# Talking heads attention with a gated MLP on one core: the first head mix of two groups at once, on four 64x64 tiles

## Chip, cores and metric

The kernel runs on one core of a Trainium2 chip. The metric is the device time of one execution in microseconds (us). Views of the trace count from the first instruction of the profiled execution.

## The reference

Four batches, 12 heads, 448 positions, head size 64. Two mixes over heads stand around the softmax; the result goes through a gated MLP with a residual.

```python
scores = scale * np.matmul(q, k.transpose(0, 1, 3, 2))
scores = np.einsum('bhij,hg->bgij', scores, w_pre)        # first head mix
scores = scores - np.max(scores, axis=-1, keepdims=True)
attn = np.exp(scores)
attn = attn / (np.sum(attn, axis=-1, keepdims=True) + 1e-09)
attn = np.einsum('bhij,hg->bgij', attn, w_post)           # second head mix
attn_out = np.matmul(attn, v)
...
h = gelu(x @ w_in); u, v = halves of h; v_n = layer norm of v, times g_ln
v_s = np.einsum('ts,bsd->btd', w_sg, v_n) + b_sg[None, :, None]
return x + (u * v_s) @ w_out
```

## The kernel before

Most fp32 values are carried as a high and a low fp16 part, so that a product takes several fp16 matmuls that add up in PSUM.

**Scores.** The 448 query rows of a batch are cut into chunks of 120, 120, 88 and 120 rows. For each chunk and head two matmuls (`qk_mm`, L674 and L675) give 120 x 448 scores. ScalarE or VectorE casts them to a high fp16 part (`qk_hi`, L695 through the helper at L291 or L293), VectorE computes the low part (`qk_lo`, L700), and for every two heads `write` (L706) sends both to a buffer `s1_d` in DRAM. There the rows of one query are 12 high rows, then 12 low rows. The first chunk of all (`N_Q32` = 1) keeps its scores in fp32 instead (L709).

**Groups.** Ten query rows are a group; a chunk has 12 groups, or 9. `load_pair` (L764) brings two groups back into one of three buffers `g`: a group as two halves of five query rows, each half with 5 x 2 x 12 = 120 partitions (query row, high or low, head). All these transfers are issued by SyncE (SP), in order.

**First head mix.** `premix` (L782) multiplies by a block matrix of `w_pre`: 120 rows, and 60 columns of 64. For each of the high and low parts of the weights and each half, one fp16 matmul of 448 columns goes to its 64 partitions of one PSUM bank (L792). The products low x low are in it, so there are four terms. In the fp32 chunk one full fp32 matmul does a group (L788).

**Softmax and second mix.** VectorE takes the maximum (`softmax_max`, L797), ScalarE the exponential with its sum (L804), VectorE the reciprocal (L809, L810). For the first 45 groups only the second weights are normalized (`w_norm`, L812) and an fp32 matmul mixes (L847); later groups are normalized and split into high and low parts, mostly on GpSimd (L293, L296), and mixed by fp16 matmuls of 64 rows that write two banks of `at2` (`postmix`, L857). Attention times v (`av`, L973) and the MLP of the batch (L1008) follow.

**Order.** `Plan` writes the order of all engines while the kernel is built: every step is a generator that yields an engine, a cost in ns, a rank (about the number of the group) and conditions; the planner picks by earliest start and rank. `slot(n)` (L880) holds the steps of group n, and adds the next group's once its own mix is placed. The two score banks (`ps_s2`, two buffers) serve the groups in turn:

```python
t = yield "pe", 746 if i < N_Q32 else 421, n - 3.5, 0, lambda: after([seen(("pair", pair_of[n])), past("exp", n - 2)])
premix(n)
```

Of the kernel before, what the change touches and what calls it, by code (L numbers as in the profile page):

```python
# [85 lines left out]
def talking_heads_gmlp(ctx, tc, q, k, v, w_pre, w_post, w_in, g_ln, w_sg, b_sg, w_out, out):  # L86
# [48 lines left out]
    wpre_hi = const.tile([2 * NH * H, 64], F16, name="wpre_hi")  # L135
    wpre_lo = const.tile([2 * NH * H, 64], F16, name="wpre_lo")
    wrep = const.tile([P, 2, H], F32, name="wrep")
    msk = const.tile([P, 5, NH], F32, name="msk")
# [14 lines left out]
    gring = [const.tile([2 * NH * H, 4, S], F16, name=f"g{i}") for i in range(RING)]  # L153
    vn_hi = const.tile([P, NCH, DH], F16, name="vn_hi")
    wfull = vn_hi.rearrange("p c f -> p (c f)")[:NT * H, 128:384].bitcast(F32)
    wpc32 = vn_hi.rearrange("p c f -> p (c f)")[:, 384:504].bitcast(F32)
    mskc_t = vn_hi.rearrange("p c f -> p (c f)")[:, 504:520].bitcast(F32)
    wpre32 = vn_hi.rearrange("p c f -> p (c f)")[:NT * H, :128].bitcast(F32)
# [21 lines left out]
    s1_d = [dram.tile([CQ * 2 * H, S], F16, name=f"s1_d{i}") for i in range(3)]  # L180
# [496 lines left out]
    def qk_full(i, h, ps, eng=None):  # L677
        ev = min(CQ, q_rows(i)[1])
        qk_place(i, h)
        e = ebox[i, h // 2 * 2].rearrange("p t u j -> p (t u j)").bitcast(F32).rearrange("p (u j) -> p u j", u=2)  # L680
        cast(e[:ev, h % 2, :], ps[:ev, :S], 1.0 / math.sqrt(D), eng)

    def qk_place(i, h):
        if h % 2 == 0:
            if (i, h) in early:
                ebox[i, h] = early[i, h].rearrange("p (t u j) -> p t u j", t=2, u=2)
# [16 lines left out]
    def s1_full(i):
        return s1_d[i % 3].rearrange("(q t) j -> q (t j)", t=2).bitcast(F32)
# [56 lines left out]
    def g_full(p):  # L761
        return gring[p % RING].rearrange("p u j -> p (u j)").bitcast(F32).rearrange("p (u j) -> p u j", u=2)

    def load_pair(p):  # L764
        i, t, n = pairs_[p]
        ng = min(2, GROUPS[chunks[i][1]] - t)
        r0 = t * NT * 2 * H
        if i < N_Q32:
            r0 = t * NT * H
            src = s1_full(i)[r0:r0 + ng * NT * H, :].rearrange("(u m) j -> m u j", m=NT * H)  # L770
            nc.sync.dma_start(out=g_full(p)[:, :ng, :], in_=src)
            return
        src = s1_d[i % 3][r0:r0 + ng * NT * 2 * H, :].rearrange("(u m) j -> m u j", m=2 * NH * H)
        nc.sync.dma_start(out=gring[p % RING][:, :2 * ng, :], in_=src)
# [4 lines left out]
    def cstart_end(i):  # L779
        return cstart[i] if i < len(chunks) else NG  # L780

    def premix(n):  # L782
        g = gring[pair_of[n] % RING]
        u = 2 * (glist[n][2] % 2)
        ps = ps_s2.tile([P, 512], F32, tag="s2", name="ps_s2")
        st[n] = {"s2": ps}
        if n < cstart_end(N_Q32):
            nc.tensor.matmul(ps[:, :S], lhsT=wfull, rhs=g_full(pair_of[n])[:, glist[n][2] % 2, :], start=True, stop=True)  # L788
# [718 lines left out]
```

## Time and profile before

| | us |
|---|---|
| three executions, median | 692.51 |
| their lowest and highest | 688.84, 981.43 |
| the profiled execution | 688.67 |
| its span, first to last instruction | 686.9 |
| TensorE busy, share of the span | 623.3 (91%) |
| VectorE, ScalarE, GpSimd busy | 474.7, 467.5, 416.7 |
| mean granted TensorE clock | 0.973 |

One of the three executions, 981.43, lies far from the other two. A matmul's duration in the profile holds its way through the array, so durations of neighbours overlap; the distance from one start to the next tells what a matmul costs the engine. `PE` is TensorE's matmuls and `PEld` its weight loads, `DVE` is VectorE, `ACT` ScalarE, `POOL` GpSimd, and `SPq` is the sequencer of SyncE, which issues the transfers.

### The profile page before, as it was taken

The page shows a single profiled execution, that of the slowest core. Times are in us where ns is not written, and L with a number is a line of the kernel's source. Part 1 is how long each engine was busy: PE and PEld are TensorE (multiplying, and loading weights), DVE is VectorE, ACT ScalarE, POOL GpSimd, SP SyncE. Part 2 cuts the span into 40 slices and gives each one's busy share as a digit, 9 for nine tenths or more (in the row PEclk, how much of TensorE's full clock was granted, in tenths as well). Part 3 has the DMA queues.
Part 4 walks back from the last instruction along what each step waited for, and adds up shares of the span by engine and source line. Part 5 has one row for each costly group of instructions (what it writes and reads, how often), then busy time and mean ns, then how long its engine had stood idle before and what let it go on. Part 6 is the DMA issues. An engine that isn't in the chain of part 4 may idle for free.

```text
span 686.9 us, 21481 instructions
## 1 busy us (share of the span) xinstructions
PE 623.3 (91%) x8589; PEld 415.2 (60%) x8589; DVE 474.7 (69%) x1073; ACT 467.5 (68%) x1037; POOL 416.7 (61%) x560
## 2 busy tenths in 40 slices
PE   6598798879779897999999998999899999999997
PEld 3355565557546644766675654775665746767776
DVE  5677998878799876756769667556768686344670
ACT  4557686768779786666778787766779696664311
POOL 5043685565679866676778767776676768773000
PEclk8889999999989998899999999999999999999999
DMA  8799999999989599766979399967887394540022
GB/s 194 211 267 277 276 269 240 279 217 293 290 231 247 129 235 248 187 189 158 280 173 239 98 249 254 194 190 201 233 176 192 103 266 129 145 130 29 1 94 80
DMA packets 152290, 135.57 MB, mean 197 GB/s; under 512 B 65646, under 2 KB 144814, under 8 KB 152190
## 3 DMA queue, kind: packets, MB, share of 16 engines
q1 hardware_dynamic: 151929, 134.19, 78.4%
q8 instruction: 67, 1.10, 0.7%
q14 instruction: 34, 0.27, 0.1%
q10 hardware_dynamic: 260, 0.01, 0.0%
HBM read 77.01 MB, written 47.87 MB: 182 GB/s over the span
## 4 chain that ended last, share of the span: by engine, by line
PE 54%; DMA 20%; DVE 12%; issue 5%; POOL 5%; ACT 3%; SPq 0%; POOLq 0%; ACTq 0%; DVEq 0%
PE ps_x L1008 10%; PE ps_av L973 7%; PE ps_s L792 7%; PE at L857 6%; PE ps_u L1008 5%; DMA g<-s_d 5%; PE ps_v L1008 5%; DMA qT<-q 5%; PE ps_qk L674 4%; PE ps_qk L675 3%; DMA s_d<-s 3%; DMA st<-in_moe_w_out_dram 2%; DVE s L700 2%; DVE nm L797 2%; PE at L847 2%
## 5 line engine op out<-in xcount | busy, mean ns | idle before, releaser
L797 DVE TENSOR_REDUCE nm<-ps_s 128x1 f32<-128x448 f32 x180 | 110.1, 615 | 42.7 <-PE ps_s L792 34.8
L296 POOL TENSOR_TENSOR pl<-p,ph 128x448 f16<-128x448 f32 x123 | 129.9, 1058 | 8.7 <-ACT ph L291 2.8
L804 ACT ACTIVATE p<-ps_s,nm 128x448 f32<-128x448 f32 x180 | 113.1, 629 | 27.1 <-DVE nm L797 24.0
L291 ACT ACTIVATE at<-at 112x480 f32<-112x480 f32 x180 | 109.8, 612 | 18.5 <-PE at L857 10.4
L700 DVE SCALAR_TENSOR_TENSOR s<-ps_qk,s 120x448 f16<-120x448 f32 (+1 forms) x172 | 105.9, 617 | 16.3 <-ACT s L291 14.0
L291 ACT ACTIVATE s<-ps_qk 120x448 f16<-120x448 f32 (+2 forms) x169 | 91.2, 542 | 21.7 <-PE ps_qk L675 19.3
L973 PE MATMUL ps_av<-at,v 112*64 112x120 f32 (+1 forms) x1536 | 83.6, 267 | 5.2 <-DVE s L700 3.1
L674 PE MATMUL ps_qk<-kT,qT 128*128 128x448 f16 (+1 forms) x192 | 71.7, 374 | 16.1 <-DVE xTl L986 11.2
L973 PEld LDWEIGHTS ps_av<-at,v 112*64 112x64 f32 x1536 | 77.5, 141 | 10.8 <-DVE s L700 3.7
L293 POOL TENSOR_SCALAR p<-p,rs 128x448 f32<-128x448 f32 x74 | 49.7, 672 | 46.9 <-DVE rs L810 28.4
L857 PEld LDWEIGHTS <-ph 64*128 64x128 f16 x2160 | 49.8, 94 | 41.6 <-issue 27.8
L792 PE MATMUL ps_s<-g,wpre_hi 120*64 120x448 f16 x336 | 64.5, 379 | 10.4 <-DMA g<-s_d 9.6
L293 POOL TENSOR_SCALAR ph<-p 128x448 f16<-128x448 f32 x100 | 59.4, 594 | 21.0 <-PE at L857 7.4
L675 PE MATMUL ps_qk<-kT,qTs 128*128 128x448 f16 (+1 forms) x192 | 69.8, 364 | 0.0
L1008 PE MATMUL ps_u<-xTh,wbuf 128*128 128x120 f16 (+1 forms) x768 | 63.6, 215 | 1.1 <-DVE gl_v L1052 1.1
L1008 PEld LDWEIGHTS <-wbuf 128*128 128x128 f16 x1152 | 59.3, 99 | 8.5 <-issue 5.7
L857 PE MATMUL at<-wpc_hi,ph 64*128 64x60 f16 x1080 | 61.4, 191 | 2.1 <-ACT at L291 2.0
L792 PE MATMUL ps_s<-g,wpre_lo 120*64 120x448 f16 x336 | 61.2, 359 | 0.0
L857 PE MATMUL at<-wpc_hi,pl 64*128 64x60 f16 x1080 | 59.9, 188 | 0.7 <-POOL pl L296 0.7
L857 PE MATMUL at<-wpc_lo,ph 64*128 64x60 f16 x1080 | 60.0, 188 | 0.0
L1008 PE MATMUL ps_u<-xTl,wbuf 128*128 128x120 f16 (+1 forms) x384 | 59.9, 215 | 0.0
L1008 PE MATMUL ps_x<-wbuf,gt_hi 128*120 128x384 f16 (+1 forms) x232 | 57.2, 329 | 0.0
(238 smaller groups left out, 1351.8 us busy)
## 6 DMA issues: line engine op xcount, KB each, us to landing
g<-s_d SPq DMA_DIRECT2D x88, 420.0 KB
s_d<-s SPq DMA_DIRECT2D x62, 420.0 KB
s_d<-s SPq DMA_DIRECT2D x24, 336.0 KB
wbuf<-wo_d SPq DMA_DIRECT2D x16, 384.0 KB
v<-in_v_dram SPq DMA_DIRECT2D x16, 336.0 KB
wbuf<-wu_d SPq DMA_DIRECT2D x12, 384.0 KB
out_dram<-ot SPq DMA_DIRECT2D x24, 180.0 KB
q<-in_q_dram SPq DMA_DIRECT2D x11, 384.0 KB
```

The costliest lines, as they stand in the source:

```text
L291: e.activation(out=o, in_=i, func=AF.Copy, scale=scale)
L293: e.tensor_scalar(out=o, in0=i, scalar1=scale, scalar2=1.0, op0=ALU.mult, op1=ALU.mult)
L296: (e or pl.on).tensor_tensor(out=o, in0=a, in1=b, op=ALU.subtract)
L674: nc.tensor.matmul(ps[:rows, :S], lhsT=qT2[i % 2][:, h, :rows], rhs=kT[:, h, :], start=True, stop=False)
L675: nc.tensor.matmul(ps[:rows, :S], lhsT=qTs2[i % 2][:, h, :rows], rhs=kT[:, h, :], start=False, stop=True)
L700: nc.vector.scalar_tensor_tensor(out=e[:ev, 1, h % 2, :], in0=ps[:ev, :S], scalar=1.0 / math.sqrt(D), in1=e[:ev, 0, h % 2, :], op0=ALU.mul ...
L792: nc.tensor.matmul(ps[64 * hf:64 * hf + 64, :S], lhsT=w, rhs=g[:, u + hf, :], start=(i == 0), stop=(i == 1))
L797: nc.vector.tensor_reduce(out=nm, in_=st[n]["s2"][:, :S], axis=AX.X, op=ALU.max, negate=True)
L804: nc.scalar.activation(out=x["p32"], in_=x["s2"][:, :S], func=AF.Exp, bias=x["nm"], accum_out=x["ss"])
L857: nc.tensor.matmul(at2[:, hf, jc * w:(jc + 1) * w], lhsT=l[rows, js], rhs=r[rows], start=(k == 0), stop=(k == 2))
L973: nc.tensor.matmul(ps[a * D:(a + 1) * D, k3 * rows:(k3 + 1) * rows], lhsT=x[:, h, jc, :], rhs=y[:, jc, h, w:w + rows], start=(jc == 0 and ...
L1008: nc.tensor.matmul(o, lhsT=l, rhs=r, start=(first and i == 0), stop=(last and i == n - 1))
```

## The change

Each half of a group (five query rows x 12 heads) now takes 60 partitions, and its high and low parts lie side by side in the free dimension of the same partition, in the score tiles, in DRAM and in `g`. The two halves of a group sit on partitions 0 to 59 and 64 to 123. The mix is done for two groups at once: three terms (high weights x high scores, high x low, low x high), each as four matmuls, one for each half of each group, with 60 rows and 64 columns. Of the second group of a pair the halves are swapped in the score bank, so that each of the four matmuls has rows and columns of its own. Since the second group's halves are swapped, its normalized weights (`w_norm`) are written in two halves, and its second mix writes the two banks of `at2` the other way round. A generator `all_premix` places the mix of a pair when both exponentials of the pair before are placed; the planner counts 913 or 720 ns for a pair instead of 746 or 421 for a group. A pair is loaded by two transfers instead of one; a write has one dimension less.

```diff
-    gring = [const.tile([2 * NH * H, 4, S], F16, name=f"g{i}") for i in range(RING)]
+    gring = [const.tile([P, 2, 2, S], F16, name=f"g{i}") for i in range(RING)]
-    s1_d = [dram.tile([CQ * 2 * H, S], F16, name=f"s1_d{i}") for i in range(3)]
+    s1_d = [dram.tile([CQ * H, 2 * S], F16, name=f"s1_d{i}") for i in range(3)]
...
     def write(i, h, r0, r1):
-        if i < N_Q32:
-            src = ebox[i, h - 1][r0:r1].rearrange("p t u j -> p (t u j)").bitcast(F32).rearrange("p (u j) -> p u j", u=2)
-            nc.sync.dma_start(out=s1_full(i).rearrange("(q n) j -> q n j", n=H)[r0:r1, h - 1:h + 1, :], in_=src)
-        else:
-            dst = s1_d[i % 3].rearrange("(q t n) j -> q t n j", t=2, n=H)
-            nc.sync.dma_start(out=dst[r0:r1, :, h - 1:h + 1, :], in_=ebox[i, h - 1][r0:r1])
+        dst = s1_d[i % 3].bitcast(F32).rearrange("(q n) j -> q n j", n=H)
+        src = ebox[i, h - 1].rearrange("p u t j -> p (u t j)").bitcast(F32).rearrange("p (u j) -> p u j", u=2)
+        nc.sync.dma_start(out=dst[r0:r1, h - 1:h + 1, :], in_=src[r0:r1])
...
     def load_pair(p):
         i, t, n = pairs_[p]
         ng = min(2, GROUPS[chunks[i][1]] - t)
+        src = s1_d[i % 3].bitcast(F32)[t * NT * H:(t + ng) * NT * H, :].rearrange("(u f m) j -> f m u j", f=2, m=NH * H)
+        for f in range(2):
+            nc.sync.dma_start(out=g_full(p)[64 * f:64 * f + NH * H, :ng, :], in_=src[f])
...
+    def premix(p):
+        i, t, n = pairs_[p]
+        g = gring[p % RING]
+        ns = sorted((m for m in range(n, min(n + 2, NG)) if pair_of[m] == p), key=lambda m: glist[m][2])
+        for m in sorted(ns):
+            st[m] = {"s2": ps_s2.tile([P, 512], F32, tag="s2", name="ps_s2")}
         if i < N_Q32:
+            terms = (wpre32, g_full(p)),
+        else:
+            terms = (wpre_hi, g[:, :, 0]), (wpre_hi, g[:, :, 1]), (wpre_lo, g[:, :, 0])
+        for k, (w, x) in enumerate(terms):
+            for u, m in enumerate(ns):
+                for f in range(2):
+                    o, rows = 64 * (f ^ u), slice(64 * f, 64 * f + NH * H)
+                    nc.tensor.matmul(st[m]["s2"][o:o + 64, :S], lhsT=w[rows], rhs=x[rows, u, :],
+                                     start=(k == 0), stop=(k == len(terms) - 1))
+        return sorted(ns)
+
+    def all_premix():
+        for p, (i, _, n) in enumerate(pairs_):
+            t = yield "pe", 913 if i < N_Q32 else 720, n - 3.5, 0, lambda: after([seen(("pair", p)), past("exp", n - 1), past("exp", n - 2)])
+            for m in premix(p):
+                tm["pre", m] = t
+                pl.add(slot(m, t))
...
     def w_norm(n):
         x = st[n]
         x["wp"] = wpp.tile([P, H * NT], F32, tag="wp", name="wp")
-        cast(x["wp"], wpost, x["rs"])
+        if glist[n][2] % 2 == 0:
+            cast(x["wp"], wpost, x["rs"])
+            return
+        for k in range(2):
+            o, w = (y.rearrange("p (g b t) -> p g b t", g=H, b=2) for y in (x["wp"], wpost))
+            cast(o[:, :, k], w[:, :, 1 - k], x["rs"])
...
-                    nc.tensor.matmul(at2[:, hf, jc * w:(jc + 1) * w], lhsT=l[rows, js], rhs=r[rows],
+                    nc.tensor.matmul(at2[:, hf ^ glist[n][2] % 2, jc * w:(jc + 1) * w], lhsT=l[rows, js], rhs=r[rows],
...
-        for n, cm, base in ((0, 2 * H, 0), (1, H, 0), (2, H, 64), (3, H, 0), (4, H, NH * H)):
+        for n, cm, base in ((0, H, 0), (1, H, 64)):
...
+        for i, w in enumerate((w_pre, w_post)):
+            for hf in range(2):
+                nc.scalar.dma_start(out=wrep[hf * 64:hf * 64 + NH * H, i, :], in_=bass.AP(
+                    tensor=w.tensor, offset=w.offset, ap=[[0, NH], [H, H], [1, H]]))
```

## Rows read from the trace of the kernel before

**Rows 1.** The page: span, and busy time, share and instructions of each engine.
```profile
span 686.9 us, 21481 instructions
PE 623.3 (91%) x8589; PEld 415.2 (60%) x8589; DVE 474.7 (69%) x1073; ACT 467.5 (68%) x1037; POOL 416.7 (61%) x560
```

**Rows 2.** Busy time by stage: stretch, its length, engines with counts, clock, DMA share, GB/s.
```profile
core 0: us, PE busy (x) PEld busy (x) DVE busy (x) ACT busy (x) POOL busy (x), PEclk, DMA share, GB/s
270.00:620.00 350.00, 336.75 (x5324) 220.63 (x5325) 227.39 (x536) 255.02 (x565) 250.34 (x318) 0.98 0.76 190
65.00:270.00 205.00, 177.59 (x2228) 118.65 (x2225) 174.32 (x380) 156.63 (x358) 137.85 (x184) 0.98 1.02 247
```

**Rows 3.** The chain that ended last, by line: 270 to 630 us, then 65 to 270.
```profile
by line: PE ps_x L1008 15.1%; PE ps_av L973 12.8%; PE ps_s L792 11.8%; PE at L857 10.6%; PE ps_v L1008 7.4%; PE ps_u L1008 6.8%; DMA g<-s_d 6.5%; PE ps_qk L674 5.8%; PE ps_qk L675 3.7%; issue 2.9%; DMA st<-in_k_dram 2.0%; DMA out_dram<-ot 1
...
by line: DMA qT<-q 14.1%; issue 12.2%; DMA st<-in_moe_w_out_dram 8.1%; DVE s L700 4.8%; DVE nm L797 4.4%; POOL pl L296 4.2%; PE at L847 4.2%; DMA gbuf<-in_moe_w_in_dram 3.6%; PE ps_s L792 3.0%; PE ps_u L1008 2.5%; POOL gt_lo L296 2.0%; DVE 
```

**Rows 4.** TensorE's order of time: start, duration, line, tiles, shapes, count. One group.
```profile
354.50 0.35 PE L675 MATMUL ps_qk<-kT,qTs 128*128 128x448 f16 x1
354.78 0.38 PE L792 MATMUL ps_s<-g,wpre_hi 120*64 120x448 f16 x2
355.00 0.36 PE L792 MATMUL ps_s<-g,wpre_lo 120*64 120x448 f16 x2
355.28 0.36 PE L674 MATMUL ps_qk<-kT,qT 128*128 128x448 f16 x1
355.48 0.35 PE L675 MATMUL ps_qk<-kT,qTs 128*128 128x448 f16 x1
355.67 0.22 PE L1008 MATMUL ps_u<-xTh,wbuf 128*128 128x120 f16 x1
```

**Rows 5.** The same view: two groups of the first mix one behind the other.
```profile
64.81 0.38 PE L792 MATMUL ps_s<-g,wpre_hi 120*64 120x448 f16 x2 [0.90 <-DMA g<-s_d]
65.02 0.36 PE L792 MATMUL ps_s<-g,wpre_lo 120*64 120x448 f16 x2
65.21 0.36 PE L792 MATMUL ps_s<-g,wpre_hi 120*64 120x448 f16 x2
65.40 0.35 PE L792 MATMUL ps_s<-g,wpre_lo 120*64 120x448 f16 x2
65.69 0.39 PE L674 MATMUL ps_qk<-kT,qT 128*96 128x448 f16 x1
```

**Rows 6.** The same view: three of the second mix's twelve steps of two matmuls.
```profile
354.12 0.19 PE L857 MATMUL at<-wpc_hi,ph 64*128 64x60 f16 x2
354.15 0.19 PE L857 MATMUL at<-wpc_lo,ph 64*128 64x60 f16 x2
354.18 0.19 PE L857 MATMUL at<-wpc_hi,pl 64*128 64x60 f16 x2
```

**Rows 7.** L792 alone by stage: stretch, length, matmuls, weight loads, clock, DMA, GB/s.
```profile
270.00:620.00 350.00, 59.80 (x420) 16.28 (x420) 0.98 0.76 190
65.00:270.00 205.00, 35.21 (x248) 10.32 (x244) 0.98 1.02 247
```

**Rows 8.** TensorE's order of time: a group of the fp32 chunk and its successor.
```profile
60.74 0.92 PE L788 MATMUL ps_s<-g,vn_hi 120*128 120x448 f32 x2
61.49 0.35 PE L674 MATMUL ps_qk<-kT,qT 128*96 128x448 f16 x1
```

**Rows 9.** The page's queue of SyncE: packets, MB, share of 16 DMA engines' span.
```profile
q1 hardware_dynamic: 151929, 134.19, 78.4%
```

**Rows 10.** Waits: who for whom, us in total, times, longest.
```profile
DVE nm L797 <- PE ps_s L792: 34.8, 39, 2.7
PE ps_s L792 <- DMA g<-s_d: 9.6, 7, 2.3
```

**Rows 11.** Issues on SyncE: count, ns least/median/most, first and last start.
```profile
L712 SPq DMA_DIRECT2D s_d<-s x86: 556/886/5201, 45.4 to 576.9; - x86
...
L709 SPq DMA_DIRECT2D s_d<-wbuf x3: 316/406/1067, 17.7 to 21.0; - x3
...
L771 SPq DMA_DIRECT2D g<-s_d x6: 329/491/1137, 28.6 to 49.7; - x6
```

**Rows 12.** All engines' order of time at the start, with idle time and its end.
```profile
7.01 0.60 ACT L1338 ACTIVATE qT<-at 128x512 f16<-128x512 f32 x1 [4.73 <-PE at L1354]
...
8.67 1.20 POOL L1364 TENSOR_SCALAR at<-at 112x768 f16<-112x768 f32 x1 [4.89 <-DMA at<-in_k_dram]
...
26.64 1.16 DVE L700 SCALAR_TENSOR_TENSOR gt_hi<-ps_qk,gt_hi 120x448 f16<-120x448 f32 x2 [0.86 <-ACT gt_hi L291]
```

**Rows 13.** Groups by line: count, busy us, mean ns, idle before. The normalized second weights.
```profile
L293 POOL TENSOR_SCALAR wp<-wpost,rs 128x120 f32<-128x120 f32 x40 | 18.3, 458 | 47.1 <-DVE rs L810 34.4 <-PE at L847 3.9 <-PE ps_s L792 3.5
```

**Rows 14.** Groups by line: maximum, exponential, and the reading of its sum.
```profile
L804 ACT ACTIVATE p<-ps_s,nm 128x448 f32<-128x448 f32 x180 | 113.1, 629 | 27.1 <-DVE nm L797 24.0 <-DVE rs L809 2.7
L797 DVE TENSOR_REDUCE nm<-ps_s 128x1 f32<-128x448 f32 x180 | 110.1, 615 | 42.7 <-PE ps_s L792 34.8 <-PE ps_s L788 7.3
...
L804 ACT ACTIVATION_READ_ACCUMULATOR p<-ps_s,nm 128x1 f32 x180 | 36.6, 203 | 0.0
```

**Rows 15.** TensorE's order of time: one block of attention times v.
```profile
307.54 2.04 PE L973 MATMUL ps_av<-at,v 112*64 112x88 f32 x48
```

More of the change, by code (lines that the diff above doesn't have):

```diff
@@ L134, in talking_heads_gmlp @@
     ident_x = const.tile([P, P], F16, name="ident_x")
-    wpre_hi = const.tile([2 * NH * H, 64], F16, name="wpre_hi")
-    wpre_lo = const.tile([2 * NH * H, 64], F16, name="wpre_lo")
+    wpre_hi = const.tile([P, 64], F16, name="wpre_hi")
+    wpre_lo = const.tile([P, 64], F16, name="wpre_lo")
     wrep = const.tile([P, 2, H], F32, name="wrep")
-    msk = const.tile([P, 5, NH], F32, name="msk")
+    msk = const.tile([P, 2, NH], F32, name="msk")
     wpost = const.tile([P, H * NT], F32, name="wpost")
@@ L685, in qk_place @@
             if (i, h) in early:
-                ebox[i, h] = early[i, h].rearrange("p (t u j) -> p t u j", t=2, u=2)
+                ebox[i, h] = early[i, h].rearrange("p (u t j) -> p u t j", t=2, u=2)
             else:
@@ L766, in load_pair @@
         ng = min(2, GROUPS[chunks[i][1]] - t)
-        r0 = t * NT * 2 * H
-        if i < N_Q32:
[L769 to L774, printed above, removed]
-    st = {}
-    def cstart_end(i):
-        return cstart[i] if i < len(chunks) else NG
@@ L782, in premix @@
[L782 to L788, printed above, removed]
-            return
-        for i, w in enumerate((wpre_hi, wpre_lo)):
-            for hf in range(2):
-                nc.tensor.matmul(ps[64 * hf:64 * hf + 64, :S], lhsT=w, rhs=g[:, u + hf, :],
-                                 start=(i == 0), stop=(i == 1))
+        src = s1_d[i % 3].bitcast(F32)[t * NT * H:(t + ng) * NT * H, :].rearrange("(u f m) j -> f m u j", f=2, m=NH * H)
@@ L878, in talking_heads_gmlp, with slot @@
     W_NORM = {"act": 197, "dve": 192, "pool": 344}, {"act": 197, "dve": 192}
-    def slot(n):
-        b, c, t = glist[n]
+    def slot(n, t):
+        b, c, _ = glist[n]
         i = NCH * b + ORD.index(c)
-        t = yield "pe", 746 if i < N_Q32 else 421, n - 3.5, 0, lambda: after([seen(("pair", pair_of[n])), past("exp", n - 2)])
-        premix(n)
-        tm["pre", n] = t
-        if n + 1 < NG:
-            pl.add(slot(n + 1))
         t = yield "dve", 531, n - 3, t
@@ L1320, in early_loads @@
                     fetch_v(0, sum(y[0] == "v" for y in tm), 0)
-        nc.scalar.dma_start(out=wrep[:2 * NH * H, 0, :], in_=bass.AP(
-            tensor=w_pre.tensor, offset=w_pre.offset, ap=[[0, 2 * NH], [H, H], [1, H]]))
-        for hf in range(2):
-            nc.scalar.dma_start(out=wrep[hf * 64:hf * 64 + NH * H, 1, :], in_=bass.AP(
-                tensor=w_post.tensor, offset=w_post.offset, ap=[[0, NH], [H, H], [1, H]]))
+        for i, w in enumerate((w_pre, w_post)):
+            for hf in range(2):
+                nc.scalar.dma_start(out=wrep[hf * 64:hf * 64 + NH * H, i, :], in_=bass.AP(
+                    tensor=w.tensor, offset=w.offset, ap=[[0, NH], [H, H], [1, H]]))
         early_loads("d" * PD0 + "v" * PV0)
@@ L1425, in talking_heads_gmlp @@
         turn_q(1, [eng[y] for y in TQ1])
-        R0 = 2 * NH * H
+        mskc = mskc_t[:, :NH]
+        nc.vector.tensor_tensor(out=mskc, in0=msk[:, 0, :], in1=msk[:, 1, :], op=ALU.add)
         nc.vector.tensor_tensor(
-            out=wpre32[:, :NH * H].rearrange("p (i g) -> p i g", i=NH),
-            in0=wrep[:R0, 0:1, :].to_broadcast([R0, NH, H]),
-            in1=msk[:R0, 0, :].unsqueeze(2).to_broadcast([R0, NH, H]), op=ALU.mult)
-        for hf in range(2):
-            nc.vector.tensor_tensor(
-                out=wfull[:, 64 * hf:64 * hf + NH * H].rearrange("p (i g) -> p i g", i=NH),
-                in0=wrep[:R0, 0:1, :].to_broadcast([R0, NH, H]),
-                in1=msk[:R0, 3 + hf, :].unsqueeze(2).to_broadcast([R0, NH, H]), op=ALU.mult)
+            out=wpre32[:, :NH * H].rearrange("p (i g) -> p i g", i=NH), in0=wrep[:, 0:1, :].to_broadcast([P, NH, H]),
+            in1=mskc.unsqueeze(2).to_broadcast([P, NH, H]), op=ALU.mult)
         nc.vector.tensor_copy(out=wpre_hi, in_=wpre32)
@@ L1450, in talking_heads_gmlp @@
             in0=wrep[:, 1, :].unsqueeze(2).to_broadcast([P, H, NT]),
[L1451 to L1453 removed]
+            in1=msk[:, 0:2, :].rearrange("p a b -> p (a b)").unsqueeze(1).to_broadcast([P, H, NT]), op=ALU.mult)
         wpc = wpc32.rearrange("p (g t) -> p g t", t=NH)
@@ L1472, in misc @@
             nc.vector.tensor_scalar(out=ident_x, in0=ident, scalar1=S_ID, scalar2=None, op0=ALU.mult)
-        for x in (slot(0), all_qk(), all_pairs(3), load_q(2), load_kv(), load_weights(), misc(), all_av(), units()):
+        for x in (all_premix(), all_qk(), all_pairs(3), load_q(2), load_kv(), load_weights(), misc(), all_av(), units()):
             pl.add(x)
```

20 lines of the change are left out of this document (7 added, 13 removed).

## The prediction, made before the changed kernel was run

> **What bounds the kernel now.** I read the page's busy shares first [rows 1]. TensorE is busy 91% of the span and no other engine over 69%, but matmul ends are modelled and the share is a mean over stages, so the table by stage comes next [rows 2]. From 270 to 620 us TensorE is busy 336.75 of 350 us while VectorE, ScalarE and GpSimd lie between 227 and 255; the DMA engines are at 0.76. From 65 to 270 us it is another kernel: TensorE 177.59 of 205, VectorE 174.32, and a DMA share of 1.02, that is a full queue (weights, q and k come in beside the scores). Third, the chain that ended last, in the same two stretches [rows 3]: from 270 to 630 us the eight matmul lines shown hold 74% of it (15.1 + 12.8 + 11.8 + 10.6 + 7.4 + 6.8 + 5.8 + 3.7), and the first head mix, L792, 11.8%; from 65 to 270 us L792 holds 3.0%, and DMA lines lead. So a microsecond of TensorE is worth most of itself late and little early.
>
> **The matmuls of the mix.** Today a group is two weights times two column halves, 448 columns each. Starts, not durations, give the cost [rows 4]. The first weight's two halves start at 354.78, the second's at 355.00, the next instruction at 355.28: 0.50 us. Before it the step from 354.50 to 354.78 is 0.28, where the same instruction takes 0.19 before an ordinary matmul (355.48 to 355.67): 0.09 goes into changing the tile shape, and of the last step of 0.28 another 0.09. A group costs 0.50 + 0.09 = 0.59 us, a pair 1.18. Where two groups stand together [rows 5] the inner steps are 0.19 and the shape changes are paid once: 0.88 + 0.09 = 0.97. That is the lower bound; the blocks that I looked at in the late stretch stand alone, so I take 1.18.
>
> After the change a pair is three steps of four matmuls. Each matmul has 60 rows and 64 columns of its own, so each quarter of the array has one. If the four go together a step is 0.19, and the pair 0.22 + 0.19 + 0.28 + 0.09 = 0.78 us (first, middle and last step and entry, as measured today). The trace doesn't show four at once. It shows two column halves at once, since a step of two at 448 columns takes 0.19, like one full matmul of 448 columns in [rows 4], and two row halves at once in the second mix [rows 6]: pairs of 60-column matmuls start 0.03 us apart, and 60/448 of 0.19 is 0.025. The upper bound is that only two go together: six steps, 0.22 + 4 x 0.19 + 0.28 + 0.09 = 1.35. I take 0.78, because both halvings run at full rate alone and the four tiles of a step share no quarter and no half bank. Saved: 0.40 us a pair.
>
> There are 420 matmul records of either weight together from 270 to 620 us, four to a group: 105 groups, 52.5 pairs, and 248 records from 65 to 270: 31 pairs [rows 7]. Late: 52.5 x 0.40 = 21 us of TensorE time, times 74% that is matmul on the chain, 15.5. Early: 31 x 0.40 = 12.4, of which I take a sixth, 2 (L792 has 3.0% of the chain there).
>
> **The fp32 chunk.** The first chunk's groups are one full fp32 matmul each, 0.75 us from 60.74 to 61.49 [rows 8]. Four fp32 tiles at once give about 0.75 + 0.02 + 2 x 0.09 = 0.95 a pair for 1.50. Six pairs: 3.3 us, in a stretch of DMA waits; between 0 and 3.3 I take 1.5.
>
> **The score transfers.** High and low parts side by side double the runs. A load of two groups was 480 runs of 896 bytes and becomes 240 of 1,792 in two transfers; a write of 120 rows was 240 runs of 1,792 and becomes 120 of 3,584. Bytes stay. The queue's mean is 0.784 x 16 x 686.9 / 151,929 = 57 ns of one engine a packet [rows 9]; no row splits it into a part by packet and a part by byte. If all of it went by packet, some 82 x 240 + 86 x 120 = 30,000 fewer packets would take 106 us off 539 us of DMA time, 20%; if all by byte, nothing. The DMA lines on the chain from 65 to 270 us that are shown are 14.1 + 8.1 + 3.6% of 205, 53 us: a fifth would be 10 us. Between 0 and 10 I take 3, nearer the bytes. Loads that TensorE itself awaited cost 9.6 us in 7 waits [rows 10]: between 0 and 9 I take 2.
>
> SyncE issues one more transfer a pair, 0.49 us by the median of the fp32 load, and the write loses a dimension: 0.89 falls to the 0.41 of the fp32 form [rows 11]. 92 x 0.49 = +45, 86 x 0.48 = -41: nothing in sum. Behind the second half load wait the writes and loads of the queue, about 0.5 us later; the ring of three pairs covers that, and without the cover it is 0.5 us at each of the 7 waits, 3.5 us. At the start one more weight transfer on ScalarE's queue, six GpSimd mask operations fewer and two VectorE products fewer lie ahead of waits [rows 12]: 4.73 us of ScalarE for TensorE, 4.89 of GpSimd for k, 0.86 of VectorE for ScalarE. The normalized weights of odd fp32 groups become two operations instead of one: at most 22 x 0.458 = 10 us more [rows 13], on GpSimd, which is busy 138 of 205 us early; uncovered it would sit ahead of the second mix. The second mix writes its two banks swapped for odd groups, with the same instructions. I take nothing for these.
>
> **The new wait.** A pair's mix needs both score banks, so it waits for both exps of the pair before; today a group needs only the exp two back. Behind a waiting mix in TensorE's order stand second mixes, score matmuls of the next chunk, attention times v and the MLP; ScalarE's evacuations wait for those, and VectorE's maximum for the mix itself. One round is mix 0.7, two maxima 2 x 0.615, the last exp 0.629 + 0.203 [rows 14] and about 0.3 for three handoffs by my estimate: 3.1 us. A pair comes every 350 / 52.5 = 6.7 us, so 3.6 us are left for queueing: one whole attention-times-v block of TensorE takes 2.0 us [rows 15], a VectorE or ScalarE item 0.6. Mostly it is covered; between nothing and 16 (the first rival below) I take a loss of 4. The order of the work is written at build time from the planner's costs; it now counts 720 ns for a pair that I put at 780, where it counted 421 for a group of 590, so the order it writes should fit the chip a little better, which I price at nothing.
>
> **Sum.** 15.5 + 2 + 1.5 + 3 + 2 - 4 = 20 us. The profiled execution took 688.67 us with a span of 686.9; the two runs that agree with it have 688.84 and 692.51, a middle of 690.7, 2 us higher. 688.67 - 20 = 668.7, and put at that middle 671.
>
> **Rivals.**
> *The round becomes the pace.* If queueing in a round passes 3.6 us, the mix is late, the maxima and exps after it too, and the second mix of the pair holds TensorE. For it: today VectorE already idles 34.8 us in 39 waits for the mix [rows 10], with two banks in turn. Against it: the mix may run 3.5 groups ahead. A round of 7.0 for 6.7 costs 52.5 x 0.3 = 16 us, and 4 of the 20 are left: 687.
>
> *Four tiles don't go together* (the change then doesn't do what it says). Place: L792's steps. The two row halves of a group write the two halves of one bank; today's row halves write two banks [rows 6], and today's halves of one bank have all rows [rows 4], so no row shows this mix. At 1.35 a pair it is 0.17 more than today: late 52.5 x 0.17 x 0.74 = 6.6, early a sixth of 31 x 0.17, 0.9, and the fp32 pair at 1.70 for 1.50, half of 6 x 0.2, 0.6. With 4 for the round and -5 for the transfers, 690.7 + 7.1 gives 698. A pair is three steps and 0.21 of ends, so it decides where a step costs over (1.18 - 0.21) / 3 = 0.32 us. The Trainium skill, TensorEngine Tiling (Array Packing), Gotcha 1: PSUM Pressure, says that different row tiles cannot access the same PSUM bank simultaneously. By that rule a pair costs 1.35 and the time is this rival's 698; by the rows of the two halvings it is 0.78 and 671. No row here shows the rule at work.
>
> *More than the forecast.* The transfers reach their bounds (10 and 9), all 21 late us and 3.3 of the fp32 chunk count, and the round is covered: 690.7 - (21 + 2 + 3.3 + 10 + 9) = 645; halfway to the forecast, 658. For it: the DMA share of 1.02 early; against it: the chain's DMA lines there are mostly others than the scores'.
>
> **How the numbers follow.** Forecast (660 to 682): 0.55. Round becomes the pace (682 to 693): 0.20. Not together (690 to 715): 0.12. More (645 to 660): 0.13. The range of 652 to 692 leaves out the third case and half of the fourth; the forecast's own range is 660 to 682. About 2% is what a measurement of this kernel can tell from no change: below 677 against 690.7. Faster by over 2%: the fourth case and 0.42 of the first, 0.55. Slower by over 2%, above 704: half of the third, 0.06. Within: 0.39.
>
> **What would show it.** Starts of the mix: three steps of 0.19 in a pair of 0.78, right; 0.38, the second rival. VectorE's wait for the mix, 34.8 us today: far above that, and TensorE idle for exps ahead of the mix, the first rival. Busy DMA share from 65 to 270 us below 1.02 and fewer than 125,000 packets. SyncE's issue of a write near 0.41. I'd be wrong outright if the late stretch lost its TensorE bound: busy shares of 270 to 620 us well under 0.9 with the same end.

## The result, and the profile after

The changed kernel took 685.39 us (median of 19 executions, 677.47 to 693.16), the kernel before 691.54 beside it: a ratio of 0.9908, 95% interval 0.9886 to 0.9931. That is 6 us or 0.9% where the forecast was 20 us or 2.8%. The profiled execution took 683.63 us with a span of 681.9. Ratios, here and below, compare executions of one session without the slow ones, so they aren't exactly quotients of the medians. Two halves have to be explained: the matmuls of the mix became as short as forecast, and most of the time did not come out at the end.

The page of the changed kernel: span, engines, and the queue of SyncE (packets, MB, share).

```profile
span 681.9 us, 22364 instructions
PE 613.6 (90%) x8949; PEld 417.0 (61%) x8949; DVE 469.6 (69%) x1066; ACT 464.4 (68%) x1048; POOL 424.4 (62%) x569
...
q1 hardware_dynamic: 122925, 134.19, 75.3%
```

TensorE's busy time fell by 9.7 us [rows 1], about twice the span. The queue has 29,000 fewer packets [rows 9], and its time went from 0.784 x 686.9 = 539 us to 0.753 x 681.9 = 513.

TensorE's order of time in the changed kernel, late: three pairs of the mix with their neighbours.

```profile
342.56 0.19 PE L864 MATMUL at<-wpc_hi,pl 64*128 64x60 f16 x2
342.68 0.57 PE L786 MATMUL ps_s<-g,wpre_hi 60*64 60x448 f16 x8
343.08 0.36 PE L786 MATMUL ps_s<-g,wpre_lo 60*64 60x448 f16 x4
343.37 0.43 PE L1010 MATMUL ps_v<-wv_hi,xTh 128*120 128x512 f16 x1
...
347.86 0.57 PE L786 MATMUL ps_s<-g,wpre_hi 60*64 60x448 f16 x8
348.26 0.36 PE L786 MATMUL ps_s<-g,wpre_lo 60*64 60x448 f16 x4
348.55 0.36 PE L673 MATMUL ps_qk<-kT,qT 128*128 128x448 f16 x1
...
354.82 0.19 PE L864 MATMUL at<-wpc_hi,pl 64*128 64x60 f16 x2
354.94 0.57 PE L786 MATMUL ps_s<-g,wpre_hi 60*64 60x448 f16 x8
355.35 0.36 PE L786 MATMUL ps_s<-g,wpre_lo 60*64 60x448 f16 x4
355.64 0.36 PE L673 MATMUL ps_qk<-kT,qT 128*128 128x448 f16 x1
```

Two steps of four matmuls take 355.35 - 354.94 = 0.41 us, the third, with the change of shape behind it, 0.29, and before it goes another 0.09 (the step from 354.82 to 354.94 is 0.12, where a step of the second mix takes 0.03 [rows 6]): a pair costs 0.79 us. Before, a group alone cost 0.59, so a pair 1.18 [rows 4]. The blocks shown are the usual ones: from the first matmul of a mix to the next other matmul the median from 270 to 620 us is 0.69 us over the 53 pairs that stand alone, and in the kernel before 0.50 over the 99 groups that stand alone.

Busy time by stage in the changed kernel, in the columns of [rows 2].

```profile
270.00:620.00 350.00, 334.03 (x5771) 227.56 (x5767) 229.74 (x550) 262.21 (x593) 255.67 (x323) 0.99 0.75 196
65.00:270.00 205.00, 174.95 (x2255) 120.42 (x2257) 173.59 (x379) 153.70 (x356) 144.51 (x197) 0.95 0.92 239
```

Late, TensorE is as full as it was. Early, the DMA share fell from 1.02 to 0.92, and TensorE's busy time is about the same, 174.95 for 177.59. The granted clock of the early stretch, a mean over its two levels of 2.4 and 1.2 GHz, is 0.95 for 0.98: by my estimate that is worth about 0.03 x 205 = 6 us of TensorE's time there.

Waits of the changed kernel from 66 us on: who for whom, us in total, times, longest. L786 mixes the fp32 chunk too, which ends before 66 us; [rows 10] holds the fp16 groups alone.

```profile
DVE nm L799 <- PE ps_s L786: 23.1, 24, 3.1
PE ps_s L786 <- DMA g<-s_d: 2.8, 4, 1.1
```

VectorE waits 23.1 us for the mix where it waited 34.8, and the mix's own wait for loads fell from 9.6 to 2.8 us.

How far the softmax had come sorts the loss by place. I take from both traces the start of the 73rd and of the 175th of the 180 readings of an exponential's sum (L804 before, L806 after; [rows 14]):

| us | before | changed | difference |
|---|---|---|---|
| start to 73rd reading | 265.1 | 274.0 | +8.9 |
| 73rd to 175th | 343.2 | 330.8 | -12.4 |
| 175th to the end of the span | 78.6 | 77.1 | -1.4 |

The late stretch gave 12.4 us, about what was forecast for it. The early stretch gave 8.9 us of it back.

### The profile page after: what moved, and what is told of

It is laid out like the page before. It is cut to its first block, busy times and chain, and to the rows that moved or that the text cites. A ratio compares the mean times of both kernels' runs of the same rounds, so it can differ in the third digit from the quotient of the medians.

```text
span 681.9 us, 22364 instructions
## 1 busy us (share of the span) xinstructions
PE 613.6 (90%) x8949; PEld 417.0 (61%) x8949; DVE 469.6 (69%) x1066; ACT 464.4 (68%) x1048; POOL 424.4 (62%) x569
## 3 DMA queue, kind: packets, MB, share of 16 engines
q1 hardware_dynamic: 122925, 134.19, 75.3%
## 4 chain that ended last, share of the span: by engine, by line
PE 47%; DVE 18%; DMA 15%; ACT 8%; issue 6%; POOL 4%; SPq 1%; ACTq 0%; POOLq 0%; DVEq 0%
PE ps_x L1010 10%; PE ps_v L1010 6%; PE ps_s L786 5%; PE ps_av L975 5%; PE ps_u L1010 5%; PE at L864 5%; DMA g<-s_d 4%; DMA s_d<-s 4%; PE ps_qk L673 3%; DVE s L699 3%; PE at L854 3%; DVE nm L799 3%; PE ps_qk L674 2%; ACT p L806 2%; DMA st<-in_k_dram 2%
## 5 line engine op out<-in xcount | busy, mean ns | idle before, releaser
L295 POOL TENSOR_TENSOR pl<-p,ph 128x448 f16<-128x448 f32 x125 | 131.3, 1052 | 12.8 <-ACT ph L290 7.3
L806 ACT ACTIVATE p<-ps_s,nm 128x448 f32<-128x448 f32 x180 | 113.1, 631 | 21.7 <-DVE nm L799 19.6
L799 DVE TENSOR_REDUCE nm<-ps_s 128x1 f32<-128x448 f32 x180 | 105.2, 615 | 26.3 <-PE ps_s L786 26.3
L290 ACT ACTIVATE s<-ps_qk 120x448 f16<-120x448 f32 (+2 forms) x170 | 91.3, 541 | 18.3 <-PE ps_qk L674 14.1
L292 POOL TENSOR_SCALAR p<-p,rs 128x448 f32<-128x448 f32 x80 | 54.1, 677 | 64.8 <-DVE rs L812 30.5
L975 PEld LDWEIGHTS ps_av<-at,v 112*64 112x64 f32 x1536 | 76.0, 140 | 10.3 <-DVE xTl L988 4.3
L292 POOL TENSOR_SCALAR ph<-p 128x448 f16<-128x448 f32 x92 | 55.0, 598 | 16.3 <-ACT p L290 6.7
L1010 PE MATMUL ps_u<-xTh,wbuf 128*128 128x120 f16 (+1 forms) x768 | 64.1, 216 | 1.1 <-DVE gl_v L1054 1.1
L1010 PEld LDWEIGHTS <-wbuf 128*128 128x128 f16 x1152 | 59.9, 100 | 6.5 <-issue 3.9
L786 PE MATMUL ps_s<-g,wpre_hi 60*64 60x448 f16 x672 | 55.7, 370 | 8.2 <-ACT p L806 5.0
L811 DVE TENSOR_SCALAR rs<-ss 128x1 f32<-128x1 f32 x180 | 26.8, 149 | 50.7 <-ACT p L806 48.2
L1010 PE MATMUL ps_u<-xTl,wbuf 128*128 128x120 f16 (+1 forms) x384 | 60.4, 216 | 0.0
L864 PE MATMUL at<-wpc_hi,pl 64*128 64x60 f16 x1080 | 59.7, 187 | 0.7 <-POOL pl L295 0.7
L864 PE MATMUL at<-wpc_lo,ph 64*128 64x60 f16 x1080 | 59.7, 187 | 0.0
L854 PE MATMUL at<-wp,p 128*112 128x120 f32 x360 | 49.6, 285 | 10.6 <-ACT at L290 7.1
```

Source lines behind the costliest of these rows:

```text
L290: e.activation(out=o, in_=i, func=AF.Copy, scale=scale)
L292: e.tensor_scalar(out=o, in0=i, scalar1=scale, scalar2=1.0, op0=ALU.mult, op1=ALU.mult)
L295: (e or pl.on).tensor_tensor(out=o, in0=a, in1=b, op=ALU.subtract)
L786: nc.tensor.matmul(st[m]["s2"][o:o + 64, :S], lhsT=w[rows], rhs=x[rows, u, :], start=(k == 0), stop=(k == len(terms) - 1))
L799: nc.vector.tensor_reduce(out=nm, in_=st[n]["s2"][:, :S], axis=AX.X, op=ALU.max, negate=True)
L806: nc.scalar.activation(out=x["p32"], in_=x["s2"][:, :S], func=AF.Exp, bias=x["nm"], accum_out=x["ss"])
```

## Experiments: is it a part of the change in the first batch?

First theory: something that the change adds in the first batch costs the 9 us: the weights normalized in two operations, the wait for two score banks, or the second load of a pair. Rival: the mix itself gains less than its blocks show. Of the first four runs three undo one or two parts in the first batch, and the fourth undoes the mix of pairs in all of them. Their expectations go by the exponential of group 30, whose reading starts at 124.0 us in the kernel before and at 134.4 in the changed one (groups count from 0, so the 73rd reading is group 72's).

**One operation for the normalized weights.** A swapped copy of the weights is made once, and odd groups use it. The copy lies in the tile of `b_sg`, whose load waits until the first batch no longer needs it.

```diff
-        for k in range(2):
-            o, w = (y.rearrange("p (g b t) -> p g b t", g=H, b=2) for y in (x["wp"], wpost))
-            cast(o[:, :, k], w[:, :, 1 - k], x["rs"])
+        cast(x["wp"], wpost_sw if glist[n][2] % 2 else wpost, x["rs"])
...
```

> The changed kernel, but an odd group's normalized weights are again one operation, from a second constant that holds them with halves swapped (it lies in the tile of b_sg, which is loaded after the first batch). Theory S (the split operation lies ahead of the second mix and costs the first 45 groups their 10 us): exp of group 30 near 124 to 127 us, time near 676 us. Theory W (the pair's wait for both exps costs the 10 us): exp of group 30 stays at 131 to 134 us, time 683 to 685. Theory O (only another order of work): no systematic change, 680 to 690.

685.01 us, ratio 0.9945 (0.9911 to 0.9978); the reading of group 30 starts at 133.0 us, and the 73rd stands 9.2 us behind before. Without the split the time does not come back. Groups of the changed kernel by line and shape, the normalized weights (count, busy us, mean ns):

```profile
L292 POOL TENSOR_SCALAR wp<-wpost,rs 128x60 f32<-128x60 f32 x36 | 14.8, 426 | 16.4 <-DVE rs L812 15.3 <-PE at L854 1.0
L292 POOL TENSOR_SCALAR wp<-wpost,rs 128x120 f32<-128x120 f32 x21 | 9.4, 450 | 36.7 <-DVE rs L812 31.9 <-PE ps_q L326 3.4 <-PE ps_s L786 1.2
```

Half the columns, in 12 pieces of five, take 426 ns and all of them 450, so a split does add nearly a whole operation on GpSimd, as the prediction had counted it. Taking it out gained nothing that the end shows.

**First batch mixed one group at a time** (two tiles a step, with the new layout), and the same **without the swap and the split**. The first part below is in both runs, the second in the second run alone, which also normalizes all weights of the first batch in one operation.

```diff
+            if i < NCH:
+                for m in range(n, min(n + 2, NG)):
+                    if pair_of[m] != p:
+                        continue
+                    t = yield "pe", 850 if i < N_Q32 else 620, m - 3.5, 0, lambda: after([seen(("pair", p)), past("exp", m - 2)])
+                    premix_one(m)
+                    tm["pre", m] = t
+                    pl.add(slot(m, t))
+                continue
...
-                o, rows = 64 * (f ^ u), slice(64 * f, 64 * f + NH * H)
+                o, rows = 64 * (f), slice(64 * f, 64 * f + NH * H)
```

> The changed kernel, but in the first batch (45 groups) the mix is done group by group, two tiles at once, when the exp two back is placed; the split weights stay. A group then costs TensorE 0.78 us, 1.56 a pair, so 16 pairs pay 0.78 us more, 13 us of TensorE time in a stretch where about a sixth counts. Theory W: the 10 us come back less 2, exp of group 30 near 125 to 127 us, time near 677. Theory S: exp of group 30 at 133 to 136, time 685 to 688. Theory O: 680 to 690 with no pattern.

> As before, group by group in the first batch, and there without swapped halves, so that one operation normalizes the weights: neither the pair's wait nor the split is left early. W and S both expect the early 10 us back less 2 for the two-tile mix: exp of group 30 near 124 to 127, time 676 to 678. If the early loss is neither (O, or the transfers) it stays at 683 to 688.

683.68 us, 0.9907 (0.9866 to 0.9948), and 684.84, 0.9916 (0.9881 to 0.9951). The reading of group 30 starts at 130.2 and 127.2 us: without the pair's wait, the swap and the split 7 of the 10 us are back by then. But the 73rd reading is 13.3 and 11.5 us behind before, so the lag arises again behind it. All three times lie where the third theory of the expectations puts them, another order of work.

**All groups one at a time** (the first edit of the run before, with `if True`): three terms, the new layout, two tiles at a time in every batch.

> The changed layout and three terms, but every group mixed by itself, two tiles at once, in all batches. If the four tiles together are what the late stretch gains by, 52.5 pairs cost 0.78 us more each, 41 us, times 0.74: 30 us, time 710 to 725 and TensorE fuller late. If the gain after 270 us comes from the transfers or from the order, time 685 to 695.

710.78 us, ratio 1.0319 (1.0239 to 1.0398), 25 us slower than the changed kernel, as expected (710 to 725). TensorE's order of time in this kernel:

```profile
304.92 0.57 PE L781 MATMUL ps_s<-g,wpre_hi 60*64 60x448 f16 x4
305.32 0.35 PE L781 MATMUL ps_s<-g,wpre_lo 60*64 60x448 f16 x2
305.61 0.27 PE L1239 MATMUL ps_x<-ident_x,xTh 128*120 128x128 f16 x1
```

One group takes 0.69 us here, the changed kernel's two take 0.70. Four tiles at once thus do twice the work of two in the same time, and that reaches the end of the kernel: this is the part of the change that pays. The rival falls.

**First batch wholly as before**: old layout, four terms, one load a pair, both kinds of mix in one kernel.

```diff
+            if i < OLD:
+                for m in range(n, min(n + 2, NG)):
+                    if pair_of[m] != p:
+                        continue
+                    t = yield "pe", 746 if i < N_Q32 else 421, m - 3.5, 0, lambda: after([seen(("pair", p)), past("exp", m - 2)])
+                    premix_old(m)
...
```

> The changed kernel, but the whole first batch (45 groups) runs as in the kernel before: its layout, writes and single loads, its mix by groups with four terms, its unswapped weights; the other three batches are as changed. If the changed parts themselves lose the time of the first batch, the late gain of 15 us stays whole: exp of group 48 within 2 us of the kernel before, of group 72 too, time 672 to 676. If the early lag does not come from them, because work is only paid earlier or later until 270 us and the lag arises after group 54 in any case, exp of group 72 is 8 to 12 us late again and the time 682 to 686.

676.2 us, 0.9779 (0.9693 to 0.9864). The time is about that of the first case, 672 to 676, but the 73rd reading, in an execution of 681.24 us, was still 7.0 us behind before, where that case has 2. The time looked like the answer, but each edit above also makes the planner write another order, so I measured what an order alone is worth.

**Two loads a pair, in the kernel before.**

```diff
-        nc.sync.dma_start(out=gring[p % RING][:, :2 * ng, :], in_=src)
+        for f in range(2):
+            ms = slice(f * NH * H, (f + 1) * NH * H)
+            nc.sync.dma_start(out=gring[p % RING][ms, :2 * ng, :], in_=src[ms])
```

> The kernel before, with every pair of fp16 groups loaded by two transfers of 60 partitions instead of one of 120, the same runs of 896 bytes: the extra issue on SyncE alone. If the second transfer makes the early lag, exp of group 60 is 5 to 10 us late and the time 695 to 700; if the queue takes it in, as I priced it, all stays within 2 us of 690.

691.56 us, 1.0041 (0.9994 to 1.0087): the second load costs between nothing and 0.9%.

## Experiments: the written order

Second theory: the order that the planner happens to write is worth as much as the change. Rival: a higher cost of the mix in the planner is simply right for the changed kernel. These edits change a number that the planner alone reads: the cost in ns of a mix, or the `LOOK` by which it looks past the earliest start. TensorE's instructions stay the same, 8,589 matmuls before and 8,949 in the changed kernel. But for many casts the planner also chooses among ScalarE, VectorE and GpSimd, and it chooses anew: GpSimd has 557 to 566 instructions in the kernels before and 563 to 589 in the changed ones. "Order" below means both, the order and that choice; no run parts them.

```diff
-            t = yield "pe", 913 if i < N_Q32 else 720, n - 3.5, 0, lambda: after([...])
+            t = yield "pe", 950 if i < N_Q32 else 780, n - 3.5, 0, lambda: after([...])
...
-        t = yield "pe", 746 if i < N_Q32 else 421, n - 3.5, 0, lambda: after([...])
+        t = yield "pe", 840 if i < N_Q32 else 590, n - 3.5, 0, lambda: after([...])
...
-LOOK = 100
+LOOK = 150
```

Cost 590 before, 780 after:

> The kernel before, with the planner's cost of a group's mix set to what the trace shows (590 ns for 421, 840 for 746 in the fp32 chunk): only the written order of the work can change. It measures how far the order alone moves the time. Theory O (the early lag is a chance of the order) expects several us either way, 685 to 700, and groups 30 to 72 shifted by up to 10 us; if order matters little the time stays within 2 us of 690 and the groups within 3.

> The changed kernel, with the planner's cost of a pair's mix set to 780 ns for 720 (950 for 913): order alone. As for the other order control: several us either way under theory O, 678 to 692; within 2 us of 685 if the order matters little.

Cost 480 before (746 stays in the fp32 chunk), 840 (and 1000 in the fp32 chunk) after, and a `LOOK` of 150 in both:

> The kernel before with 480 ns for 421 as the planner's cost of a group's mix: another written order, the same work. If orders scatter, the time lies anywhere from 684 to 706; if the 16 us of the run with 590 come from the size of that step, about a third of it, 695.

> The changed kernel with 840 ns for 720 as the cost of a pair (1000 for 913): a third order of the same work after 720 and 780. If the gain of 780 comes from a cost at or above what a pair takes, this stays near 674 to 678; if orders scatter, 672 to 690.

> The kernel before with a planner window of 150 ns for 100 inside which ranks decide: a neutral change of the order, no cost touched. If any other order of the kernel before is worse than its own, 695 or more; if orders scatter around it, 684 to 697.

> The changed kernel with the same window of 150 ns. If the change is worth the 20 us of the forecast whatever the order, this lies 15 to 25 us below the same edit of the kernel before; if it is worth 6 us, 3 to 10 below.

The costs 421 and 720 times 0.855 (746 and 913 stay), and a `LOOK` of 75 in both:

> The kernel before with the planner's cost of a group's mix 360 instead of 421 ns: same instructions, another written order. If the order is a draw and the order of before a good one among many, it lands between 690 and 710, above before by the spread seen so far (697, 706, 706). If before's order stands out only by chance of the three edits tried, it could as well come below 690.

> The changed kernel with the planner's cost of a pair's mix 616 instead of 720 ns, the same factor 0.855 as in the run beside it. If the changed kernel's own order is a poor one among many, it lands between 668 and 680; the difference to the run beside it is then 20 to 30 us. If higher costs are what helps (780 gave 674, 840 gave 668), it comes above 685.

> The kernel before with the planner's look-ahead 75 instead of 100 ns: same instructions, another order. By the order theory 690 to 710.

> The changed kernel with the same look-ahead of 75. By the order theory 668 to 685 and 20 to 30 us below the run beside it; if the change is worth only the 6 us measured, about 6 us below it.

Measured (the runs with 840 and with LOOK 150 are two executions each, those with other edits three to nine; the readings are as above, from one profiled execution each; the last column counts the MLP's matmuls, L1008 or L1010, that start between 65 and 200 us):

| kernel, order | median us | ratio to before | 95% | 73rd reading | 73rd to 175th | MLP 65-200 |
|---|---|---|---|---|---|---|
| before, own | 691.54 | 1 | | 265.1 | 343.2 | 133 |
| before, 360 | 687.49 | 0.9943 | 0.9886-1.0000 | 264.4 | 342.7 | 168 |
| before, 480 | 696.74 | 1.0076 | 1.0008-1.0145 | 269.6 | 349.4 | 148 |
| before, 590 | 705.90 | 1.0243 | 1.0192-1.0295 | 268.6 | 355.9 | 108 |
| before, LOOK 75 | 686.38 | 0.9898 | 0.9826-0.9970 | 261.4 | 344.3 | 165 |
| before, LOOK 150 | 706.26 | 1.0234 | 1.0162-1.0305 | 275.5 | 349.2 | 117 |
| changed, own | 685.39 | 0.9908 | 0.9886-0.9931 | 274.0 | 330.8 | 108 |
| changed, 616 | 675.53 | 0.9750 | 0.9692-0.9807 | 268.8 | 326.4 | 180 |
| changed, 780 | 674.26 | 0.9783 | 0.9727-0.9840 | 268.6 | 329.9 | 169 |
| changed, 840 | 668.00 | 0.9679 | 0.9603-0.9755 | 267.1 | 323.8 | 125 |
| changed, LOOK 75 | 675.98 | 0.9739 | 0.9673-0.9805 | 266.2 | 327.1 | 183 |
| changed, LOOK 150 | 677.53 | 0.9817 | 0.9780-0.9855 | 268.8 | 330.1 | 126 |

Three things follow. First, the order alone moves the kernel before by 3.4% (0.9898 to 1.0243) and the changed one by 2.3%; the two own orders differ by 0.9%. The rival falls: 616, below the own cost, helps the changed kernel as 780 and 840 do. My expectation for before's 360 and LOOK 75, 690 to 710, was wrong: both came out below it. The runs with 590 (685 to 700 expected), 780 (678 to 692) and 840 (672 or more) also left their ranges: orders scatter more than I had allowed. Before's own order is third of its six, the changed kernel's own the worst of its six.

Second, on like orders the change is worth more than on the two own ones. The same edit on both gives 706.26 and 677.53 with LOOK 150, 686.38 and 675.98 with LOOK 75, 687.49 and 675.53 with the cost times 0.855: 29, 10 and 12 us. I had expected 15 to 25 for the first and 20 to 30 for the other two, and missed all three. The mean ratio of the six orders is 1.007 before and 0.978 after, a difference of 2.9%, with an interval of 1.3 to 4.4% from their scatter: some 20 us. The six orders are those that I tried, not a drawn sample.

Third, it is nearly all won late. From the 73rd to the 175th reading the mean falls from 347.5 to 328.0 us, by 19.4 (14 to 25 by the scatter), and every changed kernel is below every kernel before. Up to the 73rd reading the means are 267.5 and 268.9: 1.4 us lost, by the scatter anything from 4 gained to 7 lost.

Why the changed kernel's own order is poor can be seen only in part. The early clock doesn't tell it from the others: with LOOK 150 it was 0.95 too, and the 73rd reading came 5.2 us sooner. Its early stage, in the columns of [rows 2]:

```profile
65.00:270.00 205.00, 176.01 (x2345) 123.30 (x2346) 178.33 (x387) 160.30 (x365) 144.75 (x200) 0.95 1.01 249
```

TensorE has room early, busy 174.95 of 205 us, and the MLP's matmuls can fill it. The MLP's line by stage (length, PE busy with count, PEld, clock, DMA share, GB/s) in the kernel before, in the changed one and in the changed one with LOOK 75:

```profile
65.00:200.00 135.00, 15.87 (x133) 11.01 (x134) 0.96 1.07 264
620.00:700.00 80.00, 53.13 (x486) 37.38 (x486) 0.99 0.13 38
```

```profile
65.00:200.00 135.00, 13.51 (x108) 8.79 (x108) 0.95 0.98 259
620.00:700.00 80.00, 50.16 (x437) 34.56 (x433) 1.00 0.13 38
```

```profile
65.00:200.00 135.00, 19.30 (x183) 13.44 (x183) 0.96 1.01 270
620.00:700.00 80.00, 44.49 (x396) 31.47 (x396) 0.99 0.13 38
```

The own order puts 75 fewer matmuls of the MLP there than LOOK 75 does, 19.30 - 13.51 = 5.8 us of busy time, and does them later; LOOK 75 is 9.4 us faster by the medians. The two orders with 108 are the slowest, and within 0.4 us of the slowest, of their kernels. But it doesn't sort the rest: with 125 the changed kernel is at its fastest, and 148 is slower than 133 in the kernel before. So it goes with the loss and isn't shown to be its cause. The chain of waits doesn't sort them either. Its lines from 270 to 630 us, in the changed kernel, with cost 840, and with LOOK 75:

```profile
by line: PE ps_x L1010 13.3%; PE ps_av L975 8.6%; PE at L864 8.3%; PE ps_v L1010 7.6%; PE ps_s L786 6.2%; PE ps_u L1010 6.2%; DMA s_d<-s 5.6%; issue 4.4%; PE ps_qk L673 3.7%; DVE s L699 3.2%; ACT p L806 2.8%; PE ps_qk L674 2.6%; DMA qT<-q 2
```

```profile
by line: PE ps_x L1010 14.1%; PE ps_v L1010 12.1%; PE ps_av L975 11.3%; PE at L864 10.0%; PE ps_u L1010 9.0%; PE ps_s L786 8.0%; PE ps_qk L673 4.9%; PE ps_qk L674 3.4%; issue 2.8%; DMA q<-in_q_dram 2.4%; DMA s_d<-s 2.2%; ACT at L290 2.1%; P
```

```profile
by line: PE ps_x L1010 13.8%; PE at L864 8.3%; PE ps_v L1010 8.3%; PE ps_av L975 8.0%; PE ps_u L1010 7.7%; PE ps_s L786 6.7%; DMA s_d<-s 4.5%; PE ps_qk L673 4.1%; issue 3.9%; ACT p L806 2.8%; PE ps_qk L674 2.8%; DMA qT<-q 2.7%; DMA g<-s_d 2
```

The eight matmul lines hold 56.5% in the own order, 72.8% with 840, 59.7% with LOOK 75, and 74% in the kernel before [rows 3]. The mix is down from 11.8% to between 6 and 8% in all three. The changed kernel lost part of its TensorE bound in the late stretch, but LOOK 75 has nearly the same chain and is 9 us faster. What makes one order better than another stays open.

The changed kernel with a cost of 840 is the fastest that ran: 668.00 us in two executions, 0.968 of before, faster than both kernels.

Since the experiments of the first batch also rewrote the order, their 9 us either way can't be put down to the part that they undid: 676.2 us for the first batch as before lies where other orders of the changed kernel lie. What they do show is that no part of it, taken back, made the own order's 8.9 us at the 73rd reading go away in the three runs with the new layout. Only the kernel mixed one group at a time lies outside every order of the changed kernel.

## Why the prediction was right, and where it failed

**Right: the price of the mix.** Pair 0.78 forecast, 0.79 measured; 1.18 before. The second rival (698) fell, and with it the rule that I had set against the change: the Trainium skill, TensorEngine Tiling (Array Packing), Gotcha 1: PSUM Pressure, keeps different row tiles from accessing one PSUM bank at a time. Here two row tiles write the two partition halves of one bank, in two banks at once, at 0.205 us a step: the rule doesn't hold the mix back, and the measurement decides. Over the whole kernel, the sum of distances from a mix matmul to the next matmul is 97.6 us in the mean of the six orders before and 75.6 after: 22 us, waits behind a mix included, of the 26 that 84 pairs times (1.00 - 0.69) give, without the 0.09 of entry.

**Right: packets and queue.** 122,925 packets (under 125,000), DMA share 0.92 early. Of that fall part is the own order's, which does less there: the mean of the six orders goes from 1.00 to 0.97. By the packet alone 106 us of DMA time were to go, by the byte none; 539 - 513 = 26 went. SyncE's lines of the changed kernel (least, median and most ns):

```profile
L764 SPq DMA_DIRECT2D g<-s_d x184: 315/396/2043, 29.9 to 597.3; - x184
...
L705 SPq DMA_DIRECT2D s_d<-s x88: 316/338/3541, 25.7 to 573.3; - x88
```

A write's issue fell from 0.886 to 0.338 us [rows 11]; the forecast was 0.41.

**Right: the round doesn't become the pace.** VectorE's wait for the mix fell from 34.8 to 23.1 us over the fp16 groups. With the 4 us that I took off for it the late terms were 15.5 - 4 = 11.5, and the own order gave 12.4. In the mean of the six orders it was 19.4, most of the 21 us of TensorE time: 15.5 lies in its interval of 14 to 25 and 11.5 doesn't. So the cover held; whether the weight of 74% was too low as well can't be told. The price of this rival is added up wrongly: its 687 takes 16 us for the round besides the 4 that are already in the 20. With 16 in their place it is 683.

**Wrong: the early terms, 2 + 1.5 + 3 + 2 = 8.5.** They came out as nothing: 1.4 us lost in the mean of the six orders, where the scatter leaves room for a gain of 4 at most, and 8.9 lost in the own one. I counted what the DMA engines and TensorE would be relieved of as time won, in a stage where my own view showed no one engine as the bound. The relief was real on the queue: 26 us of DMA time, and the mix's wait for loads over the fp16 groups, 6.3 to 13.3 us in the six orders before and 1.1 to 2.8 in the changed ones. The fp32 pair, priced at 0.95 with 0.09 of entry, takes 0.91 without it at its quickest, in TensorE's order of time,

```profile
56.15 0.98 PE L786 MATMUL ps_s<-g,vn_hi 60*64 60x448 f32 x8
57.06 0.39 PE L673 MATMUL ps_qk<-kT,qT 128*96 128x448 f16 x1
```

against 0.75 for one group [rows 8]. But the other five pairs stretch to between 1.44 and 2.61 us. One reason is the new wait: TensorE's weight loads for a pair's second group wait for the exponential that frees its bank, which stands in the view of waits:

```profile
PEld ps_s L786 <- ACT p L806: 3.9, 4, 1.8
```

From its first matmul to the next other matmul all six pairs hold TensorE for 11.1 us, as long as the 12 groups before, 11.0, so the fp32 term gave nothing. None of the relief reached the 73rd reading. The lines of the chain in the changed kernel, 65 to 270 us, show what stands there now:

```profile
by line: issue 10.2%; PE at L854 8.5%; DMA g<-s_d 7.7%; DVE s L699 4.8%; DVE nm L799 4.7%; PE ps_s L786 4.0%; DMA st<-in_k_dram 3.5%; DVE st L295 3.0%; ACT at L290 3.0%; ACT p L806 2.8%; PE ps_qk L673 2.5%; POOL q L295 2.0%; PE ps_qk L674 1
```

Where the chain before had 14.1% of query transfers [rows 3], this one has issue, the fp32 second mix and the score transfers: other waits stand where those transfers stood. Each is one chain of one order, so it shows what stands there and not that one took the other's place.

That the six orders give 20 us in the mean, as forecast, is luck: late some 8 us more than my 11.5, early about 10 less than my 8.5, and the rest behind the 175th reading.

**Wrong: the order "which I price at nothing".** This is the step that decided the own order's time. I wrote that it "should fit the chip a little better"; it is the worst of the six that ran. Against the mean of the other five of its kernel the own order costs 274.0 - 267.9 = 6.1 us early and 330.8 - 327.5 = 3.3 late; before's own order is 2.8 and 5.1 us better than its other five. Together that is 17 us between two orders, beside a change worth some 20. What makes an order slow stays open. With bounds of 2% either way on that one step, the 6 us would have been an ordinary outcome. As it was, 685.39 lay in the range by luck, through the case in which the round becomes the pace (687), for another reason.

## What to carry to other kernels

Where a program writes the order of a static schedule, any edit is two edits: run the kernel before and the changed one under several neutral changes of the planner's numbers, and compare the two groups, before a difference of 1 or 2% is put down to the change. Price work at the weight of its stage: in the mean of the orders, time off TensorE came out nearly whole where TensorE was full (19.4 of 21 us) and not at all where no single engine was. And once a change is in, try a few orders: here that gave some 16 us more (0.9908 to 0.9679 of before) for two costs in the planner.

## What was not expected of the hardware

Four 60x64 matmuls of 448 columns at once, two row tiles and two column tiles, took 0.41 us for two steps, as the first step of a mix (0.22) and a later one (0.19) of one group did before [rows 4, rows 5]: the packing costs nothing that these rows show. On GpSimd a multiplication of 60 columns in pieces of five took 426 ns and one of 120 columns 450, so that halving it so saves next to nothing. And 19% fewer packets with the same bytes took 5% off the DMA engines' time (539 to 513 us).
